# A matrix read whole in the last pair of a first pass, and a place of their own for the first operands of the second pass

## The chip, the cores and the metric

The kernel runs on one core of a Trainium2 chip. The metric is the device time of one execution, in microseconds (us). A core has a TensorE (PE: matrix products, with its weight loads listed apart as PEld), a VectorE (DVE), a ScalarE (ACT), a GpSimd (POOL) and a SyncE (SP), which here does nothing but issue DMAs, one after the other. Each engine works through its own list of instructions in order, and waits for others by semaphores. DMAs move data between the device memory (HBM) and the on-chip memories.

## What is computed

One transformer layer with a spatial gate, x of 2048 rows and 512 columns, all in float32:

```python
x = A_x
h = x + _A_ref(_layernorm(x, axis=-1), A_wqkv, A_wo)       # softmax attention, 32 heads of 16
h2 = h + _B_ref(_layernorm(h, axis=-1), B_w_in, B_w_sp, B_b_sp, B_w_out)

def _B_ref(x, w_in, w_sp, b_sp, w_out):                    # F = 1376, Fh = 688
    z = _gelu(jnp.einsum("bsd,df->bsf", x, w_in))
    z1 = z[..., :Fh]
    z2 = _layernorm(z[..., Fh:], axis=-1)
    g = jnp.einsum("ts,bsf->btf", w_sp, z2) + b_sp[None, :, None]
    return jnp.einsum("bsf,fd->bsd", z1 * g, w_out)
```

The change lies in the second half: the gate product `w_sp @ z2` (2048 x 2048 by 2048 x 688) and the last product with `w_out` (688 x 512).

## The kernel before

Every float32 product is made of three products of a high and a low part: a matrix is split into `hi` (a rounded copy) and `lo` (the rest), and `mm3` (L86-L90) issues hi·hi, hi·lo and lo·hi. `parts` (L757) splits for the gate stage: the copy on ACT (L762), the subtraction on DVE (L763).

The stages are: the projections; the attention (512 units, L674-L738, with a hand-written order of the engines and of SP); the stage `mid`, which makes h, z1 and z2 and stores them in HBM (`h_scr`, `z_scr`); and `fin` (from L867), the gate.

`fin` computes the gate product in the manner of Strassen and Winograd with seven half-size products. A pair `p` (0 to 7) is the row block p of the upper half and the row block p + 8 of the lower half.

- **First pass** (L903-L965): for each pair four products g7, g6, g4, g5, 24 matmuls each. `keep` (L907) makes three sums of them on DVE and stores them to `g_scr[p]` with SP (L910). The operands made of z2 stand in the tiles `T["t3"]`, `T["t2"]`, `T["n4"]`, `T["t1"]`, each as a high and a low tile, of the pool `zc`; the operands made of `w_sp` rotate through six slots of 128 x 2048 (tags w0 to w2 of pool `wc`, f0 to f2 of pool `fin_s`). In the last pair (`last`) the operands of the second pass are made as well: `a11`, `s4`, `a12` into slots f0 to f2, the rest of `b11`, and `b22` and `b21` (8 blocks each, by `load_b`, L880, and `put_b`) in the places of t3 and t2. `load_b` takes its six staging buffers in turn, three of pool `fin_1` and three with the tag `hn` of pool `early_2` (`e2`).
- **Second pass** (L1034-L1086, order of PE, ACT and DVE written by hand): for each pair three products g1, g3, g2; the sums that `fetch` (L978) loads from `g_scr` are added, the result `pr` (a top and a bottom row block, `top` and `bot`) is multiplied with z1, turned (transposed on PE, L1010, split into `pT` by L80 and L85) and multiplied with `w_out` (`wu`, 18 matmuls of 512 columns), h is added and the rows stored. `fetch(p)` loads the sums `q`, the gate rows `z1`, the rows `h`, and for p > 0 `a11`, `a12` and `s2` of `w_sp`. `fetch(0)` and `fetch(1)` are called ahead of the loop's first products.

Pools are places in the on-chip memory. `wc`, `e2` and `fin_1` belong to `late`, which is closed (L972) between the passes; the pool `fin_2` of the second pass takes the memory that they leave. An instruction that writes a tile of `fin_2` therefore waits until everything that read or wrote the old tiles in that memory is done, DMAs too. The tiles `q`, `z1`, `h`, `a11`, `pr` and `pT` of the second pass are all of `fin_2`.

`w_out` is split during the attention: for each of its six row blocks `split_wu` (L660) loads it and splits it on POOL, `store_wu` (L669) stores both parts into `w_scr` in HBM. In the last pair of the first pass the two parts of the first five blocks are loaded from `w_scr` into the place of `n4` (L957-L962), and those of the last block of 48 rows (L968-L971) into the place of the high tile of `t1`.

SP's issue order in `fin` is the scheduler's. Between the passes it is:

```
wu high part, keep(1) store, wu low part, keep(2) and keep(0) stores, wu last block x2,
fetch(0): q, z1[0], h[0], z1[1], h[1]
fetch(1): q, a11 x2, a12 x2, s2 x2, z1[0], h[0], z1[1], h[1]
fetch(2): q, ...
```

Of the kernel before, what the change touches and what calls it, by code (L numbers as in the profile page):

```python
# [8 lines left out]
F32 = mybir.dt.float32  # L9
F32R = mybir.dt.float32r  # L10
# [8 lines left out]
P = 128  # L19
S = 2048  # L20
D = 512
H = 32
DH = 16
FH = 688
# [3 lines left out]
HB = NB // 2  # L28
# [10 lines left out]
FB = [(i * P, min(P, FH - i * P)) for i in range(6)]  # L39
FC = FH // 2  # L40
# [4 lines left out]
def block_kernel(ctx: ExitStack, tc: tile.TileContext, x, wqkv, wo, w_in, w_sp4, b_sp, w_out, out):  # L45
# [7 lines left out]
    nc = tc.nc  # L53
# [3 lines left out]
    dram = ctx.enter_context(tc.tile_pool(name="dram", bufs=1, space=DRAM))  # L57
# [14 lines left out]
    z_scr = [dram.tile([S, FH], F32, name=f"z{i}_scr") for i in range(2)]  # L72
    s_scr = dram.tile([HB, P, HB, P], F32, name="s_scr")
    g_scr = [dram.tile([3, P, FC], F32, name=f"g{p}_scr") for p in range(HB)]
    w_scr = dram.tile([2, FH, D], F32, name="w_scr")

    def split(hi, lo, src, eh=None, el=None):

        if eh == "act":
            nc.scalar.activation(hi, src, AF.Copy)  # L80
        elif eh == "pool":
            nc.gpsimd.tensor_copy(hi, src)  # L82
        else:
            nc.vector.tensor_copy(hi, src)
        (nc.gpsimd if el == "pool" else nc.vector).tensor_sub(lo, src, hi.bitcast(F32))  # L85
# [161 lines left out]
    with ExitStack() as pre:  # L247
# [163 lines left out]
        with tc.manual_schedule(engines={E.PE, E.Activation, E.DVE, E.SP}):  # L411
# [47 lines left out]
            for g in range(3):  # L459
                a, b = 4 * g, 4 * g + 4  # L460
# [44 lines left out]
            for j in range(24):  # L505
                b, n, i = 1 + j // 8, j // 2 % 4, 1 - j % 2
# [28 lines left out]
    wc = late.enter_context(tc.tile_pool(name="wc", bufs=1))  # L535
    e2 = late.enter_context(tc.tile_pool(name="early_2", bufs=2))
# [54 lines left out]
    with ExitStack() as at:  # L591
# [65 lines left out]
            nc.sync.dma_start(t, src[:, a, f])  # L657
            split(dst[0][:, a, f], dst[1][:, a, f], t, "pool", "pool")

        def split_wu(i):  # L660

            f0, fn = FB[i]
            t = e2.tile([P, D], F32, name="wu", tag="hn", bufs=3)
            nc.sync.dma_start(t[:fn], w_out[f0:f0 + fn, :])
            wus[:] = [e2.tile([P, D], F32R, name=f"wu{j}", tag=f"o2{j}", bufs=1) for j in range(2)]
            split(wus[0][:fn], wus[1][:fn], t[:fn], "pool", "pool")

        def store_wu(i):
            f0, fn = FB[i]  # L669
            for j in range(2):  # L670
                nc.sync.dma_start(w_scr[j, f0:f0 + fn, :], wus[j][:fn].bitcast(F32))

        wus = []

        units = [(hg, qb, kb) for hg in range(HG) for qb in range(NQ) for kb in range(NB)]
        prev, turn, later = None, [0], []
        with tc.manual_schedule(engines={E.PE, E.Activation, E.DVE, E.SP}):
            for n in range(0, len(units), 2):
                (hg, qb, kb), (_, _, kb1) = units[n:n + 2]
                if hg + 1 < HG and n % 64 < 24 and n % 4 == 0:  # L680
                    load_k(hg + 1, [n % 64 // 4])
                if hg + 1 < HG and n % 64 < 12 and n % 4 == 2:
                    load_uv(hg + 1, [n % 64 // 4])
                if hg + 1 < HG and n % 64 == 30:
                    load_v(hg + 1)
                if kb == 2 and n // NB + 3 < HG * NQ:
                    load_q(n // NB + 3)
                steps = max_pair(m) if m < 8 * HG * NQ else []
                m += 1
                if not steps and not later:  # L690
                    maxima.close()
                    later.append(attn.enter_context(
                        tc.tile_pool(name="ps_l", bufs=1, space=PSUM, side="right")))
                step = lambda b: steps and steps.pop(0)(b)
                pts = [score(hg, qb, kb, 0), score(hg, qb, kb, 1)]
                step(2)
                step(0)
                if prev is None:

                    pv[0] = ps_v.tile([P, 512], F32, name="pv")  # L700
                    for j in range(4):
                        nc.tensor.matmul(pv[0][32 * j:32 * j + 32, :], vst[0][:, :32],
                                         vst[0][:, :512], start=True, stop=True)
                else:
                    weigh(*prev)
                step(1)
                if kb == 0 and n:
                    gather(*units[n - 1][:2])
                step(2)
                pts1 = [score(hg, qb, kb1, 0)]  # L710
                step(0)
                pts1.append(score(hg, qb, kb1, 1))
                step(1)
                step(2)
                weigh(hg, qb, kb, pts)
                if turned:
                    max_rows()
                step(1)
                prev = (hg, qb, kb1, pts1)
                if kb == 6 and n > NB:  # L720
                    invert()
                if n % 32 == 16 and n < 6 * 32:
                    load_weights(n // 32)
                if 6 * 32 <= n < 12 * 32:
                    if n % 32 == 16:
                        split_wu(n // 32 - 6)
                    if n % 32 == 26:
                        store_wu(n // 32 - 6)
                if n in (498, 502, 506):
                    load_o(h_rows[(n - 498) // 4])  # L730
                if n in (502, 506):
                    split_o(h_rows[(n - 502) // 4])
                if n in (504, 508):
                    make_h(h_rows[(n - 504) // 4], later[0].tile([P, 512], F32, name="h"), True)
            weigh(*prev)
            gather(*prev[:2])
            invert()
# [5 lines left out]
    zc = ctx.enter_context(tc.tile_pool(name="zc", bufs=1, side="right"))  # L743
# [14 lines left out]
    def parts(hi, lo, src, el=None, eh=None):  # L758
        if eh == "pool":
            nc.gpsimd.tensor_copy(hi, src)  # L760
        else:
            nc.scalar.activation(hi, src, AF.Copy)  # L762
        (nc.gpsimd if el == "pool" else nc.vector).tensor_sub(lo, src, hi.bitcast(F32))  # L763
# [36 lines left out]
    with ExitStack() as mid:  # L800
# [56 lines left out]
        w = [Slot(wc, f"w{i}") for i in range(3)]  # L857
# [15 lines left out]
    with ExitStack() as fin:  # L873
# [8 lines left out]
        def load_b(i, j, k):  # L882

            t = (f1.tile([P, FC], F32, name="b", bufs=3) if k % 2 else
                 e2.tile([P, FC], F32, name="b", tag="hn", bufs=3))
            nc.sync.dma_start(t, z_scr[1][(HB * i + k) * P:(HB * i + k + 1) * P, j * FC:(j + 1) * FC])
            return t
# [14 lines left out]
        for p in range(HB):  # L902
# [17 lines left out]
            put_b(b11, p, load_b(0, 0, p))  # L920
            if last:
                bs = [load_b(1, 1, k) for k in range(6)]
            if p:
                product(g7, ops["s3"], T["t3"])
            else:
                for blocks in (range(HB - 1), range(HB - 1, HB)):
                    product(g7, ops["s3"], T["t3"], blocks)
                    product(g6, ops["s2"], T["t2"], blocks)
# [26 lines left out]
            keep(1, g4, p67)  # L955
            if last:

                wu = [zc.tile([P, HB * FC], F32R, name="wu", tag=f"n4_{i}")[:, :5 * D].rearrange(
                    "p (a c) -> p a c", c=D) for i in range(2)]
                for i in range(2):  # L960
                    nc.sync.dma_start(wu[i].bitcast(F32),
                                      w_scr[i, :5 * P, :].rearrange("(a p) c -> p a c", p=P))  # L962
            product(g5, ops["s1"], T["t1"])
            keep(2, g5, p67)
            keep(0, g5, p6)  # L965
            ops, old, now = nxt, now, new
        fn = FB[-1][1]
        t = zc.tile([P, HB * FC], F32R, name="wu5", tag="t1_0")  # L968
        wu = [[w[:, i, :] for i in range(5)] + [t[:fn, j * D:(j + 1) * D]] for j, w in enumerate(wu)]
        for i in range(2):  # L970
            nc.sync.dma_start(wu[i][5].bitcast(F32), w_scr[i, 5 * P:, :])  # L971
        late.close()  # L972


# [2 lines left out]
        def fetch(p):  # L977

            rows = [slice((p + HB * i) * P, (p + HB * i + 1) * P) for i in range(2)]
            half = lambda n: [f2.tile([P, QB, P], F32, name=n) for _ in range(2)]  # L980
            q = f2.tile([P, 3, FC], F32, name="q")
            nc.sync.dma_start(q, g_scr[p].rearrange("i p c -> p i c"))
            raw = None
            if p:
                raw = [half("a11"), half("a12"), half("s2")]
                load_a(raw[0], 0, 0, p)
                load_a(raw[1], 0, 1, p)
                for n in range(2):
                    nc.sync.dma_start(raw[2][n], cut(s_scr[p])[n])
            z1 = [f2.tile([P, FH], F32, name=f"z1{i}") for i in range(2)]  # L990
            h = [f2.tile([P, D], F32, name=f"h{i}") for i in range(2)]
            for i in range(2):
                nc.sync.dma_start(z1[i], z_scr[0][rows[i], :])
                nc.sync.dma_start(h[i], h_scr[rows[i], :])
            return q, raw, z1, h

# [119 lines left out]
```

## Time and profile before

| what | us |
|---|---|
| three runs, median (lowest to highest) | 1916.77 (1914.2 to 1917.29) |
| the profiled execution, its own time | 1915.51 |
| its span, first to last instruction | 1913.7 |
| PE busy | 1881.6 (98%) |
| DVE busy | 1532.8 (80%) |
| ACT busy | 1326.3 (69%) |
| POOL busy | 215.5 (11%) |

The span runs from the first to the last instruction; the execution's own time is 1.8 us longer. The page cuts the span in 40 equal slices of 47.8 us and gives each engine's busy share of a slice as a digit (9 is 90% or more). PE's digits are 9 in all slices but one near the end. The matmuls are pipelined, so the start-to-start distance of two, and not the listed length of one, says how fast PE goes. PEclk is the clock granted to PE (1.00 is full).

The first pass and the second pass lie one behind the other in the last sixth of the span: in the profiled execution the last product of the first pass ends at 1714.9 us, and the second pair of the second pass starts at 1751.07 us.

### The profile page before, as it was taken

The page shows a single profiled execution, that of the slowest core. Times are in us where ns is not written, and L with a number is a line of the kernel's source. Part 1 is how long each engine was busy: PE and PEld are TensorE (multiplying, and loading weights), DVE is VectorE, ACT ScalarE, POOL GpSimd, SP SyncE. Part 2 cuts the span into 40 slices and gives each one's busy share as a digit, 9 for nine tenths or more (in the row PEclk, how much of TensorE's full clock was granted, in tenths as well). Part 3 has the DMA queues.
Part 4 walks back from the last instruction along what each step waited for, and adds up shares of the span by engine and source line. Part 5 has one row for each costly group of instructions (what it writes and reads, how often), then busy time and mean ns, then how long its engine had stood idle before and what let it go on. Part 6 is the DMA issues. An engine that isn't in the chain of part 4 may idle for free. (4 is left out here: it accounts for less than half of the span.)

```text
span 1913.7 us, 32477 instructions
## 1 busy us (share of the span) xinstructions
PE 1881.6 (98%) x11608; PEld 1067.1 (56%) x11608; DVE 1532.8 (80%) x3101; ACT 1326.3 (69%) x1729; POOL 215.5 (11%) x293
## 2 busy tenths in 40 slices
PE   9999999999999999999999999999999999996999
PEld 6765444444444444444444444444349899995887
DVE  6487999999999999999999999999536677674554
ACT  3335888888888888888888888888964345342221
POOL 2130000001011000000000000000015551001211
PEclk9999999999999999999999999999999999998999
DMA  5677111210221111121122021000045556657550
GB/s 187 185 196 184 40 24 31 70 26 28 49 51 32 38 45 27 52 46 35 35 56 44 15 53 32 22 13 5 7 106 156 160 171 206 199 182 257 181 181 34
DMA packets 151161, 165.46 MB, mean 86 GB/s; under 512 B 63256, under 2 KB 92968, under 8 KB 149464
## 3 DMA queue, kind: packets, MB, share of 16 engines
q1 hardware_dynamic: 146360, 152.11, 29.6%
q10 hardware_dynamic: 4608, 11.27, 1.5%
q8 instruction: 91, 1.49, 0.3%
q14 instruction: 70, 0.57, 0.1%
q0 software_dynamic: 32, 0.01, 0.0%
HBM read 103.98 MB, written 58.43 MB: 85 GB/s over the span
## 5 line engine op out<-in xcount | busy, mean ns | idle before, releaser
L612 ACT ACTIVATE pt<-s 128x1024 f32<-128x1024 f32 x1024 | 992.9, 1029 | 144.4 <-PE s L609 142.1
L209 DVE TENSOR_REDUCE mx<-m 128x1 f32<-128x512 f32 x1511 | 958.1, 683 | 105.6 <-PE m L204 62.3
L204 PE MATMUL m<-kst,qst 48*128 48x512 f32 x1511 | 607.5, 448 | 0.0
L620 PE MATMUL pv<-pt,vst 128*32 128x512 f32 x4096 | 550.8, 605 | 0.4 <-ACT o L627 0.4
L609 PE MATMUL s<-qst,kst 50*128 50x512 f32 x2048 | 465.9, 428 | 2.9 <-ACT pt L612 2.3
L204 PEld LDWEIGHTS m<-kst,qst 48*128 48x128 f32 x1511 | 263.5, 184 | 314.9 <-DVE mx L209 221.2
L609 PEld LDWEIGHTS s<-qst,kst 50*128 50x128 f32 x2048 | 223.0, 185 | 57.2 <-ACT pt L612 32.6
L204 PE MATMUL m<-uvs,qst 48*128 48x512 f32 x503 | 248.9, 495 | 0.0
L204 PEld LDWEIGHTS m<-uvs,qst 48*128 48x128 f32 x503 | 91.8, 183 | 207.2 <-DVE mx L209 205.3
L218 DVE CUSTOM_DVE_ANT_0 ab<-m,ab 128x512 f32<-128x512 f32 x252 | 171.2, 679 | 3.8 <-ACT ab L214 2.0
L620 PEld LDWEIGHTS pv<-pt,vst 128*32 128x32 f32 x4096 | 82.9, 108 | 161.6 <-issue 155.6
L214 ACT ACTIVATE ab<-m 128x512 f32<-128x512 f32 x251 | 150.9, 601 | 16.8 <-PE m L204 16.3
L82 POOL CAST mparts<-nm 128x16 fp32r<-128x16 f32 x32 | 6.3, 198 | 749.9 <-DVE nm L224 749.9
L762 ACT ACTIVATE ws<-a 128x512 fp32r<-128x512 f32 x80 | 46.6, 625 | 60.8 <-issue 26.7
L88 PE MATMUL acc<-wi,hT 128*128 128x344 f32 x256 | 82.9, 324 | 0.0
L89 PE MATMUL acc<-wi,hT 128*128 128x344 f32 x256 | 81.8, 320 | 0.0
L90 PE MATMUL acc<-wi,hT 128*128 128x344 f32 x256 | 81.8, 319 | 0.0
L763 DVE TENSOR_TENSOR ws<-a,ws 128x512 fp32r<-128x512 f32 x80 | 55.8, 741 | 14.4 <-ACT ws L762 14.4
L88 PE MATMUL g<-b,ws 128*128 128x344 f32 x192 | 65.0, 338 | 0.0
L80 ACT ACTIVATE pT<-tp 128x384 fp32r<-128x384 f32 (+2 forms) x48 | 18.4, 382 | 66.4 <-PE tp L1010 49.0
L88 PE MATMUL g<-t,ws 128*128 128x344 f32 x192 | 61.4, 320 | 0.6 <-issue 0.6
L89 PE MATMUL g<-b,ws 128*128 128x344 f32 x192 | 61.9, 322 | 0.0
(185 smaller groups left out, 2179.2 us busy)
## 6 DMA issues: line engine op xcount, KB each, us to landing
a<-in_w_sp SPq DMA_DIRECT2D x80, 256.0 KB
qst<-q_scr SPq DMA_DIRECT2D x192, 64.0 KB
kst<-k_scr SPq DMA_DIRECT2D x48, 256.0 KB
z_scr<-z ACTq DMA_DIRECT2D x32, 344.0 KB
k_scr<-part SPq DMA_DIRECT2D x16, 512.0 KB
q_scr<-part SPq DMA_DIRECT2D x16, 512.0 KB
z<-z_scr SPq DMA_DIRECT2D x16, 344.0 KB
b<-z_scr SPq DMA_DIRECT2D x24, 172.0 KB
```

The lines of the kernel that those rows point to most:

```text
L88: nc.tensor.matmul(ps, lh, rh, start=first, stop=False)
L89: nc.tensor.matmul(ps, lh, rl, start=False, stop=False)
L90: nc.tensor.matmul(ps, ll, rh, start=False, stop=last)
L204: nc.tensor.matmul(acc, q[r, p, c], keys[r, p], start=True, stop=True)
L209: nc.vector.reduce_max(at(t, e if t else e - 1), acc, axis=AX.X)
L214: nc.scalar.activation(ab[0], acc, AF.Abs)
L218: nc.vector.tensor_tensor_reduce(ab[0], acc, ab[0], 0.5, LOW, ALU.add, ALU.max, at(0, 0))
L609: nc.tensor.matmul(s[:, t, :], k[r, p, kb * P:(kb + 1) * P], q[r, p, :], start=True, stop=True)
L612: nc.scalar.activation(t, s, AF.Exp, scale=DH ** -0.5)
L620: nc.tensor.matmul(pv[0][32 * j:32 * j + 32, :], vst[hg % 2][:, c:c + 32], pts[j % 2][:, j // 2, :], start=kb == 0, stop=kb == NB - 1)
L762: nc.scalar.activation(hi, src, AF.Copy)
L763: (nc.gpsimd if el == "pool" else nc.vector).tensor_sub(lo, src, hi.bitcast(F32))
```

## The change

The splitting of `w_out` during the attention, with its scratch tensor in HBM, is taken out. In the last pair of the first pass `w_out` is loaded as it is: the first four row blocks by one DMA into the slot w2, the last two by one DMA each into buffers with the tag `rc` of `e2`. It is split with `parts` into the same places as before, the first two blocks ahead of the product g5, the rest behind the first pass. The sums and the z1 rows of `fetch(0)` get a place of their own, the low tile of `t1`, instead of tiles in `fin_2`. In `fetch` the z1 rows are loaded straight behind the sums, the lower row block first, and h comes last, the lower first too.

```diff
-    w_scr = dram.tile([2, FH, D], F32, name="w_scr")
...
-        def split_wu(i):
-
-            f0, fn = FB[i]
-            t = e2.tile([P, D], F32, name="wu", tag="hn", bufs=3)
-            nc.sync.dma_start(t[:fn], w_out[f0:f0 + fn, :])
-            wus[:] = [e2.tile([P, D], F32R, name=f"wu{j}", tag=f"o2{j}", bufs=1) for j in range(2)]
-            split(wus[0][:fn], wus[1][:fn], t[:fn], "pool", "pool")
-
-        def store_wu(i):
-            f0, fn = FB[i]
-            for j in range(2):
-                nc.sync.dma_start(w_scr[j, f0:f0 + fn, :], wus[j][:fn].bitcast(F32))
...
-                if 6 * 32 <= n < 12 * 32:
-                    if n % 32 == 16:
-                        split_wu(n // 32 - 6)
-                    if n % 32 == 26:
-                        store_wu(n // 32 - 6)
...
             if last:
                 bs = [load_b(1, 1, k) for k in range(6)]
+
+                raw_u = wc.tile([P, 4, D], F32, name="wr", tag="w2")
+                nc.sync.dma_start(raw_u, w_out[:4 * P, :].rearrange("(a p) c -> p a c", p=P))
+                raw_u = [raw_u[:, :2, :], raw_u[:, 2:, :]]
...
             keep(1, g4, p67)
             if last:
 
+                for f0, n in FB[4:]:
+                    t = e2.tile([P, D], F32, name="wr", tag="rc")
+                    nc.sync.dma_start(t[:n], w_out[f0:f0 + n, :])
+                    raw_u.append(t[:n])
                 wu = [zc.tile([P, HB * FC], F32R, name="wu", tag=f"n4_{i}")[:, :5 * D].rearrange(
                     "p (a c) -> p a c", c=D) for i in range(2)]
-                for i in range(2):
-                    nc.sync.dma_start(wu[i].bitcast(F32),
-                                      w_scr[i, :5 * P, :].rearrange("(a p) c -> p a c", p=P))
+                parts(wu[0][:, :2, :], wu[1][:, :2, :], raw_u[0])
             product(g5, ops["s1"], T["t1"])
...
         t = zc.tile([P, HB * FC], F32R, name="wu5", tag="t1_0")
+        wu_places = [[w[:, 2 * i:2 * i + 2, :] for w in wu] for i in range(2)]
+        wu_places += [[w[:, 4, :] for w in wu], [t[:fn, j * D:(j + 1) * D] for j in range(2)]]
         wu = [[w[:, i, :] for i in range(5)] + [t[:fn, j * D:(j + 1) * D]] for j, w in enumerate(wu)]
-        for i in range(2):
-            nc.sync.dma_start(wu[i][5].bitcast(F32), w_scr[i, 5 * P:, :])
+        for i in range(1, 4):
+            parts(*wu_places[i], raw_u[i])
+        t = zc.tile([P, HB * FC], F32, name="qz", tag="t1_1")
+        first = (t[:, :3 * FC].rearrange("p (i c) -> p i c", c=FC),
+                 [t[:, (3 + 2 * i) * FC:(5 + 2 * i) * FC] for i in range(2)])
         late.close()
...
-            q = f2.tile([P, 3, FC], F32, name="q")
+            q, z1 = first if not p else (f2.tile([P, 3, FC], F32, name="q"),
+                                         [f2.tile([P, FH], F32, name=f"z1{i}") for i in range(2)])
             nc.sync.dma_start(q, g_scr[p].rearrange("i p c -> p i c"))
+            for i in (1, 0):
+                nc.sync.dma_start(z1[i], z_scr[0][rows[i], :])
             raw = None
...
-            z1 = [f2.tile([P, FH], F32, name=f"z1{i}") for i in range(2)]
             h = [f2.tile([P, D], F32, name=f"h{i}") for i in range(2)]
-            for i in range(2):
-                nc.sync.dma_start(z1[i], z_scr[0][rows[i], :])
+            for i in (1, 0):
                 nc.sync.dma_start(h[i], h_scr[rows[i], :])
```

In the program built from it, SP's order between the passes is: `w_out` (four blocks), the three stores of pair 6, `w_out` (the last two blocks), ten `load_b`, the keep(1) store, `fetch(0)`'s q, the keep(2) and keep(0) stores, `fetch(0)`'s z1 x2 and h x2, then `fetch(1)`: q, z1 x2, a11 x2, a12 x2, s2 x2, h x2, then `fetch(2)`. The first split of `w_out` (128 x 1024) stands on DVE between the sixth and the seventh block of b21, on ACT between the fifth and the sixth, with a second one behind the sixth; the rest of them stand behind the last block of b21, on DVE behind the sums of keep(0). PE's order is as before.

More of the change, by code (lines that the diff above doesn't have):

```diff
@@ L658, in load_weights @@
             split(dst[0][:, a, f], dst[1][:, a, f], t, "pool", "pool")
-        def split_wu(i):
-            f0, fn = FB[i]
-            t = e2.tile([P, D], F32, name="wu", tag="hn", bufs=3)
-            nc.sync.dma_start(t[:fn], w_out[f0:f0 + fn, :])
-            wus[:] = [e2.tile([P, D], F32R, name=f"wu{j}", tag=f"o2{j}", bufs=1) for j in range(2)]
-            split(wus[0][:fn], wus[1][:fn], t[:fn], "pool", "pool")
-        def store_wu(i):
-            f0, fn = FB[i]
-            for j in range(2):
-                nc.sync.dma_start(w_scr[j, f0:f0 + fn, :], wus[j][:fn].bitcast(F32))
-        wus = []
         units = [(hg, qb, kb) for hg in range(HG) for qb in range(NQ) for kb in range(NB)]
```

## The prediction

> **What bounds the kernel now.** I read the slices first, to find where PE is not full; then the work by stretches of 20 and of 3 us there; then PE's waits; then the chain of waits through that place.
>
> ```profile
> PE   9999999999999999999999999999999999996999
> ...
> PEclk9999999999999999999999999999999999998999
> ```
>
> PE sets the time everywhere but in slice 36 (1722 to 1770 us), the seam between the two passes; its clock is lower there too. In stretches (us; then PE, PEld, DVE, ACT, POOL busy with counts; granted clock; DMA share; GB/s):
>
> ```profile
> 1700.00:1720.00 20.00, 20.00 (x129) 20.00 (x129) 16.11 (x34) 10.30 (x23) 0.00 (x0) 1.00 0.65 183
> 1720.00:1740.00 20.00, 7.89 (x43) 7.58 (x42) 3.33 (x6) 1.76 (x3) 0.00 (x0) 0.71 0.88 299
> 1740.00:1760.00 20.00, 16.72 (x72) 12.89 (x70) 11.08 (x21) 6.07 (x13) 4.51 (x3) 0.87 0.75 256
> 1760.00:1780.00 20.00, 20.00 (x115) 18.02 (x115) 11.53 (x20) 4.81 (x11) 3.42 (x3) 1.00 0.57 188
> ```
>
> While PE stands, the DMA engines are the busy ones. PE's longest waits in the gate stage:
>
> ```profile
> PE tp L1010 <- DVE pr L1048: 12.1, 1, 12.1
> PE acc L88 <- ACT pT L80: 3.8, 2, 3.2
> ```
>
> PE runs out at 1724.4 (its 60 products of the second pass that need no `pr`, from 1714.9, at 0.157 us each), waits 12.1 us for the first `pr`, turns it at 1736.54, runs the second half of g2, and waits 3.2 us for `pT` until 1744.70. Pair 1 starts at 1751.07. The chain (start, us, what):
>
> ```profile
> 1716.12 0.44 DVE q L909
> 1716.57 0.32 SPq L910
> 1716.94 1.77 SPq L961
> 1718.81 0.67 SPq L910
> 1719.58 9.19 DMA g_scr<-q
> 1728.85 0.38 SPq L982
> 1729.29 0.48 SPq L993
> 1729.81 0.43 SPq L994
> 1730.28 5.08 DMA z<-z_scr
> 1735.38 7.45 DMA s<-s_scr
> 1742.92 0.70 DVE s L782
> 1743.64 0.64 ACT ws L762
> ```
>
> The last `g_scr` store takes 9.19 us, because the 2.8 MB of `wu` issued around it share the DMA engines. Only then may q(0) be loaded (L982): its tile lies where the stored sums lay. Then comes z1[1] (L993), which frees the first wait, and s2 of pair 1, which frees the second: on ACT and DVE the split of pair 1's s4 stands ahead of the `pT` split. The second wait is so a refill by DMA: 14.0 us from q(0)'s issue at 1728.85 to s2's landing at 1742.83.
>
> **The change, part by part.**
>
> *Attention.* 12 POOL instructions go (six of 0.61 and six of 1.29 us, 11.4 us) and 18 DMA issues of SP. The beat of the attention, from one `mparts` of POOL to the next, starts at 666.95, 705.97, 745.07, 784.09, 823.16: 39.02 with a `wu` split in it, 39.10 without, 39.02 with, 39.07 without. The splits were hidden under PE and cost nothing; bounds -0.5 to +0.5 us over six. I take 0.
>
> *Loads of w_out in the last pair.* 1.05 MB is issued behind the `w_sp` loads that end at 1702.3; its slot w2 was last read by pair 6's g4, done at 1696.1, so SP does not wait. Queued behind it are the stores of pair 6, the last two blocks (0.36 MB, which wait for the split of a11 at 1706 to 1707.3) and ten `load_b`, the first of which waits for a DVE split at 1707.7 anyway. The DMA engines moved 153 to 203 GB/s between 1702 and 1708 and 399 elsewhere (1738 to 1741), so there is room. Lower bound 0; upper bound 1.41 MB at 158 GB/s (the stretch 1726 to 1729), 8.9 us. I take 0.5 us on the chain of `load_b`, since room is there.
>
> *Splits of w_out.* One 128 x 1024 on DVE ahead of the last sums: twice 0.60 us (the step from one 128 x 512 L763 to the next), 1.2 us; on ACT two of 1.05 (two L762 of 128 x 512: 1.14). By the order of the two engines b21's last two blocks end at 1719.1 in place of 1717.85, and keep(0) at 1720.0 in place of 1718.7; with the 0.5 above, 1720.5. The other splits (1.2, 0.6 and 0.6 on DVE) run until 1723, while the stores land. If that cover is gone they cost up to 2.4 us.
>
> *Stores of the sums.* Issued at 1720.6 to 1721. They no longer stand among 2.8 MB, only q(0)'s 0.53 MB. Bounds: 2.0 us (a `load_b` issued at 1714.4 is used at 1716.39) and 9.19. I take 2.4: landed at 1723.2. The Trainium skill ("DMA: Bandwidth & Descriptors", "Latency and other measured facts") puts the fixed cost of a DMA at about 2 us, largest when HBM is loaded; with 2.0 in place of 2.4 the sum would be 0.4 us lower.
>
> *q(0) and z1(0).* q(0) is issued behind keep(1)'s store at about 1717.3 (its place is free since g5's end at 1714.9) and lands, with the 4.1 us of before (1728.85 to 1732.95), at 1721.4. z1 follows the last store: issued 1721.0, with 3 to 5.08 us landed at 1724 to 1726. But `pr` still lies in `fin_2`, so the first DVE sum still waits for the stores: 1723.2. Three sums 1.54, the multiplication 0.88: PE turns at 1726.0 in place of 1736.54. First gap: 1.6 in place of 12.1 us.
>
> *The refill.* h(0) is now the first load that waits for the stores: 1723.2. Behind it SP issues h, q(1), z1 x2, four loads of `w_sp` and s2 x2, some 0.47 us each; all of pair 1's preparation waits for them. From h(0)'s issue to s2 0.52 + 0.53 + 0.70 + 1.05 + 0.52 = 3.3 MB, and 0.70 of z1(0) issued 2.2 us earlier: 4.0 MB; before, 3.85 MB in 14.0 us. Counted from z1(0)'s issue: 1721.0 + 14.0 x 4.0/3.85 = 1735.6; counted from h's alone 1723.2 + 14.0 x 3.3/3.85 = 1735.2; a11 in the middle, by its own 11.1 us from a11's issue (1731.75) to s2's landing, now issued at 1725.4, 1736.5. I take 1736.0 (bounds under the rivals).
>
> *Behind it* the steps stay: 1.87 us from s2's landing to PE (1742.83 to 1744.70), and 6.37 us for `bot`'s 18 products. Nine of these run at 0.43 us and nine at 0.235, as before, because PE has then stood from 1728.5 to 1737.9, and the clock fell within 4 us of standing (1.00 until 1726, 0.87 in 1726 to 1729, 0.50 after). Pair 1 starts at 1736.0 + 1.87 + 6.37 = 1744.2 in place of 1751.07: **6.8 us less**. From there all is as before; only pair 2's z1 are loaded ahead of its `w_sp`, 0.7 MB, and these are needed 7 us into pair 1.
>
> Sum: 0 (attention) - 10.5 (first gap) - 2.5 (the turn and g2's second half at full clock: 0.57 + 12 x 0.157 in place of 4.95) + 6.2 (second gap, 9.4 in place of 3.2) = -6.8. Of the profiled execution's 1915.51 (span 1913.7 and 1.8 around it) that leaves 1908.7. The median of the runs shown stands 1.3 us higher; I forecast **1909.0**.
>
> **The rivals.**
>
> *B, a fast refill.* Nothing but pair 1's operands is left to load, and 399 GB/s was moved at 1738 to 1741 and 402 behind it. 3.3 MB and 0.3 MB left of z1 at 399 take 9.0 us; from 1723.2 with 1.5 us until data flows s2 lands at 1733.7 or sooner: gain 9.1 to 11, 1905. Against it: SP issues each load alone, and before the rate was 169 GB/s in the first 3 us. The Trainium skill ("DMA: Bandwidth & Descriptors", "Where 436 GB/s comes from") sets 358 GB/s for one core's share of HBM; the trace went above that, so the row decides; with 358 B would gain 1.1 us less.
>
> *C, the stall moves whole.* The `load_b` chain ends 2 us later still, z1(1)'s 0.7 MB ahead of a11 and s2 count in full, and s2 lands 14.0 us behind the first load that `fin_2` lets go, but at 1725.2: 1739.2 to 1740. Gain 2.8 to 3.6, 1912.4.
>
> *D, slower: w_out ahead of the ten `load_b`.* Place: the loop DVE, SP, DMA, ACT, DVE through six buffers in the last pair. The sum p67 of pair 7 (1711.84) stands behind b22's last blocks, and g1 needs its bank at 1714.9, so 3 us are free; past that PE stands and the stores, the refill and pair 1 follow. It eats the gain when b22's block 6 is 7.3 us later than before (1710.06), and is a loss over 0.2% from 11 us on: 1.41 MB at 128 GB/s or less. With 14 us (100 GB/s) the end comes 6.7 us later: 1922. Against it: 153 to 248 GB/s flowed here already.
>
> *E, it doesn't do what it says.* The places help q and z1 but `pr` stays behind the stores. If these still take 9.19 us (then the cause isn't `wu`), they land at 1729.8, h is issued where q(0) was, and 1915.2 comes out. For it: nothing but the overlap shows the cause. Against it: 300 and 388 GB/s were flowing at 1720 to 1726, and the stores are 0.35 MB.
>
> **How the numbers follow.** Forecast 0.56 (own range 1906 to 1911.7), B 0.15, C 0.11, E 0.08, D 0.10. About 0.2%, 3.8 us, is what a measurement of this kernel can tell from no change. Faster by more: the forecast, B and a fifth of C, 0.73; within: the rest of C, E, a little of the other two, 0.17; slower: D, 0.10. The range 1903.5 to 1914 leaves out E, D and the far ends.
>
> **What would show it.** Right: the `g_scr` store landing in 2 to 3 us; PE's wait for L1048's successor under 3 us at 1724 to 1727; a wait of 8 to 10 us for the `pT` split ending at 1737 to 1739; PE full in the attention as before. Wrong: p67 of pair 7 later than 1714.9 (D), stores of 9 us (E), a `pT` wait of 12 us or more (C) or under 7 (B), or a gap of PE where there was none.

## The result, and the profile after

| | before | changed |
|---|---|---|
| median of 8 runs (lowest to highest), us | 1916.32 (1914.2 to 1917.29) | 1910.62 (1908.08 to 1914.73) |
| ratio to before, 95% interval | | 0.9973 (0.9962 to 0.9984) |
| the profiled execution: own time, span | 1915.51, 1913.7 | 1914.12, 1912.3 |

The kernel became faster by 5.2 us by the ratio (3.1 to 7.3), 5.7 us by the medians. The profiled execution of the changed kernel, 1914.12 us, is the second slowest of its eight. The same kernel was measured once more later (label after_again: ratio 0.9974, 0.9965 to 0.9984; median 1910.84, 1908.32 to 1914.27; its profiled execution 1909.47), and the two profiles together show what varies.

The slices of the changed kernel's page:

```profile
span 1912.3 us, 32432 instructions
...
PE   9999999999999999999999999999999999997999
...
PEclk9999999999999999999999999999999999998999
```

The seam is still the only place where PE is not full. The work by stretches (columns as before the prediction):

```profile
1700.00:1720.00 20.00, 17.29 (x102) 17.01 (x101) 12.73 (x26) 8.73 (x21) 0.00 (x0) 0.92 0.67 202
1720.00:1740.00 20.00, 12.19 (x68) 11.63 (x66) 11.43 (x21) 5.82 (x10) 0.05 (x1) 0.84 0.88 292
1740.00:1760.00 20.00, 16.89 (x74) 13.43 (x75) 11.36 (x20) 5.98 (x13) 4.44 (x3) 0.81 0.59 204
```

PE does 4.3 us more in 1720 to 1740 and 2.7 us less in 1700 to 1720: a hole has opened ahead of the old one. PE's waits (total, times, longest):

```profile
PE acc L87 <- ACT pT L79: 9.5, 2, 8.9
PE g L87 <- ACT p L924: 2.7, 1, 2.7
...
PE tp L1001 <- ACT pr L1038: 2.0, 1, 2.0
```

The 12.1 us for the first `pr` are down to 2.0. The wait for `pT` grew from 3.2 to 8.9, as worked out. New is 2.7 us at the first product of the second pass, which waits until ACT has read g6 of pair 7 (L924). The chain of waits of this execution (start, us, what) says why:

```profile
1709.07 6.70 DMA b<-z_scr
1715.79 0.49 ACT b L741
...
1724.15 0.85 DVE q L888 x2
...
1726.66 0.68 DVE wu L742
1727.36 0.32 SPq L985
...
1732.69 7.26 DMA s<-s_scr
1740.05 1.37 DVE s L761
1741.50 1.17 ACT ws L741 x2
1742.67 0.39 ACT pT L79
```

One `load_b`, b22's block 6, takes 6.70 us (2.3 before: issued at 1707.76, used at 1710.06). ACT's reading of g6 and DVE's p67 stand behind it, so PE waits, and the last sums of the pass are ready at 1725.0 instead of 1718.7. Then the split of `w_out` ends (1727.3), h(0) is issued at 1727.36, and 12.6 us later s2 of pair 1 has landed (1739.95), which frees the `pT` split.

In the second profile of the same kernel the same steps stand:

```profile
PE acc L87 <- ACT pT L79: 9.0, 2, 8.4
PE tp L1001 <- DVE pr L1039: 3.5, 1, 3.5
```

and in its chain

```profile
1705.42 6.26 DMA b<-z_scr
...
1720.07 0.85 DVE q L888 x2
...
1728.38 6.92 DMA s<-s_scr
```

The `load_b` is as slow (6.26 us), but it was issued 3.6 us earlier, while PE's first pass ended only 1.1 us earlier, and PE did not run into it. So the late `load_b` is there in both profiles, and whether PE has to wait for it depends on how far DVE and PE are apart by then. Of the 4.9 us between the two spans, 3.8 us lie in the seam and 1.1 us ahead of it. How much of the spread of the other runs (6.7 us in all) comes from this isn't shown.

### The profile page after: what moved, and what is told of

It is laid out like the page before. It is cut to its first block, busy times and chain, and to the rows that moved or that the text cites. A ratio compares the mean times of both kernels' runs of the same rounds, so it can differ in the third digit from the quotient of the medians.

```text
span 1912.3 us, 32432 instructions
## 1 busy us (share of the span) xinstructions
PE 1883.8 (99%) x11608; PEld 1068.5 (56%) x11608; DVE 1535.9 (80%) x3105; ACT 1328.8 (69%) x1733; POOL 203.9 (11%) x281
## 5 line engine op out<-in xcount | busy, mean ns | idle before, releaser
L213 ACT ACTIVATE ab<-m 128x512 f32<-128x512 f32 x251 | 151.2, 602 | 16.7 <-PE tp L203 10.5
L87 PE MATMUL g<-b,ws 128*128 128x344 f32 x192 | 65.7, 342 | 2.7 <-ACT p L924 2.7
L88 PE MATMUL g<-b,ws 128*128 128x344 f32 x192 | 62.5, 326 | 0.0
L89 PE MATMUL g<-b,ws 128*128 128x344 f32 x192 | 62.4, 325 | 0.0
```

The source lines that it names most:

```text
L87: nc.tensor.matmul(ps, lh, rh, start=first, stop=False)
L88: nc.tensor.matmul(ps, lh, rl, start=False, stop=False)
L89: nc.tensor.matmul(ps, ll, rh, start=False, stop=last)
L213: nc.scalar.activation(ab[0], acc, AF.Abs)
```

## The experiments

All compare with runs of the kernel before on the same chip. The seam of each profile, from PE's order in time, runs from the end of the first pass (the last product with t1) to the start of pair 1's first product. Each row but its median is of one execution, whose own time stands in the second column from the right.

| kernel | `load_b` of b22[6], us | wait for first pr | wait for pT | seam | from pair 1 to the end | this execution, us | median, us |
|---|---|---|---|---|---|---|---|
| before | 2.3 | 12.1 | 3.2 | 36.2 | 162.6 | 1915.5 | 1916.3 |
| changed | 6.7 | 2.7 + 2.0 | 8.9 | 35.9 | 162.6 | 1914.1 | 1910.6 |
| after_again | 6.3 | 3.5 | 8.4 | 32.2 | 162.5 | 1909.5 | 1910.8 |
| place_only | 2.35 | 12.3 | 5.9 | 39.5 | 162.7 | 1918.1 | 1915.6 |
| wout_only | 5.3 | 9.4 | 4.1 | 33.9 | 162.5 | 1914.5 | 1911.25 |
| wout_half | 2.8 | 0 | 9.2 | 27.3 | 162.5 | 1909.4 | 1912.7 |
| wout_late | 2.25 | 10.3 | 8.3 | 39.3 | 162.5 | 1913.8 | 1916.4 |
| before_pt | 2.4 | 13.0 | 0 | 32.1 | 162.6 | 1911.1 | 1908.6 |
| wout_pt | 5.9 | 6.8 | 0 | 25.8 | 162.5 | 1903.1 | 1903.5 |
| pt_first | 6.3 | 2.5 | 0 | 20.7 | 163.8 | 1899.9 | 1901.5 |

From pair 1 on nothing differs by more than 1.3 us: all that these kernels win or lose lies ahead of it. The end of the first pass itself moved between 1710.2 and 1717.8 over these profiles, which is why the seam, and not one execution's total, is compared. Most of that movement is older than the first pass: its first product started between 1589.7 (wout_late) and 1595.9 (wout_only), in kernels whose code is the same up to there. The pass itself took 120.4 to 120.6 us in each of them but wout_half, where it took 127.1.

**place_only**: the kernel before with the own place and the new order of `fetch` alone.

```diff
+        t = zc.tile([P, HB * FC], F32, name="qz", tag="t1_1")
+        first = (t[:, :3 * FC].rearrange("p (i c) -> p i c", c=FC),
+                 [t[:, (3 + 2 * i) * FC:(5 + 2 * i) * FC] for i in range(2)])
...
-            q = f2.tile([P, 3, FC], F32, name="q")
+            q, z1 = first if not p else (f2.tile([P, 3, FC], F32, name="q"),
+                                         [f2.tile([P, FH], F32, name=f"z1{i}") for i in range(2)])
             nc.sync.dma_start(q, g_scr[p].rearrange("i p c -> p i c"))
+            for i in (1, 0):
+                nc.sync.dma_start(z1[i], z_scr[0][rows[i], :])
...
-            z1 = [f2.tile([P, FH], F32, name=f"z1{i}") for i in range(2)]
             h = [f2.tile([P, D], F32, name=f"h{i}") for i in range(2)]
-            for i in range(2):
-                nc.sync.dma_start(z1[i], z_scr[0][rows[i], :])
+            for i in (1, 0):
                 nc.sync.dma_start(h[i], h_scr[rows[i], :])
```

> Only the own place for q(0) and z1(0) and the new order of fetch; w_out goes through w_scr as before. Refill theory (what ends the seam is the moment at which the memory of the late pools is let go, plus 14 us of loads): the stores still share the DMA engines with 2.8 MB and land about 9 us after their issue, h(0) is issued at 1728 to 1729, s2 of pair 1 lands at 1741 to 1742, PE's wait for the first pr falls from 12.1 to about 7 us and the wait for pT grows to 6 to 8: gain 0 to 2 us, 1914 to 1916. Place theory (the freed place of q and z1 is what shortens the seam): gain 5 us or more, about 1910.

Measured: ratio 1.0001 (0.9990 to 1.0011), median 1915.58. PE's waits, DVE's first sums for `pr` (start, length, in brackets the wait ahead of them), and two steps of its chain:

```profile
PE tp L1014 <- DMA q<-g_scr: 12.3, 1, 12.3
PE acc L88 <- ACT pT L80: 6.5, 2, 5.9
```

```profile
1733.44 1.54 DVE L1050 SCALAR_TENSOR_TENSOR pr<-g,bias,qz 128x344 f32<-128x344 f32 x3 [13.13 <-DMA qz<-g_scr]
```

```profile
1721.64 9.45 DMA g_scr<-q
...
1736.29 7.40 DMA s<-s_scr
```

With 2.8 MB of `wu` around them the stores take 9.45 us again, and h(0) is issued when they have landed, at 1731.17. The first sums of `pr` start only at 1733.44: they wait for q(0) itself. Its place was free, but its load was issued at 1723.25, behind the stores and `wu`, and landed some 10 us later. So in this kernel the own place lets q(0) be issued before the stores land, and wins nothing, since the load stands behind the same bytes. The expectation of 7 us for the first wait was too good (12.3; its last sums and stores were also 2 us later than in the profile before). The total is the refill theory's, and a gain of 5 us by the place alone is ruled out. What the place is worth without `wu` in the way, this run can't say; wout_only and wout_pt below, which leave it out, can.

**wout_only**: the changed way of `w_out` alone; q(0), z1(0) and `fetch` as before.

> Only the way of w_out is changed (loaded whole in the last pair, split there); q(0), z1(0) and fetch as before. Refill theory: the stores land 2 to 4 us after their issue, q(0) is loaded at once behind them, the first pr comes some 4 us later than with the own place, but s2 lands about 14 us behind the release all the same: gain 4 to 6 us, 1910 to 1912. Place theory: no gain, 1916 or slower by the splits, 1917.

Measured: 0.9973 (0.9961 to 0.9986), median 1911.25. The whole gain of the change comes from this part.

```profile
PE tp L997 <- DVE pr L1035: 9.4, 1, 9.4
PE acc L87 <- ACT pT L79: 4.6, 2, 4.1
```

The first wait is 6 to 7 us longer than with the own place (9.4 against 3.5 and 2.0), the second 4 to 5 us shorter, and the seam of 33.9 us lies between the two of the changed kernel: the place moves time from one wait to the other, since s2 of pair 1 ends the seam in both.

**wout_half**: three blocks of `w_out` loaded early into `fin_1`, 0.62 MB in the last pair.

```diff
+            if p == 2:
+                raw_e = f1.tile([P, 3, D], F32, name="wre", bufs=1)
+                nc.sync.dma_start(raw_e, w_out[:3 * P, :].rearrange("(a p) c -> p a c", p=P))
...
-                nc.sync.dma_start(raw_u, w_out[:4 * P, :].rearrange("(a p) c -> p a c", p=P))
+                nc.sync.dma_start(t[:, :2, :], w_out[3 * P:5 * P, :].rearrange("(a p) c -> p a c", p=P))
+                nc.sync.dma_start(t[:FB[-1][1], 2, :], w_out[5 * P:, :])
```

> The changed kernel, but three of w_out's row blocks are loaded during pair 2 into a buffer of fin_1, and only 0.62 MB instead of 1.41 MB is issued in the last pair ahead of the ten load_b. If w_out ahead of the load_b is what makes PE wait 2.7 us at the start of the second pass and delays the last sums by 5 us: that wait is gone or under 1 us, the load_b issued at 1709 lands in 2 to 4 us instead of 6.7, median 1906 to 1909 with a narrower spread. If the splits or the load_b themselves are the cause: the same as the changed kernel, 1910 to 1911, with the wait.

Measured: 0.9981 (0.9970 to 0.9992), median 1912.73; 1906 to 1909 was expected. The seam did what was expected, the total did not.

```profile
PE acc L87 <- ACT pT L79: 9.2, 1, 9.2
PE g L89 <- DVE ws L742: 3.8, 1, 3.8
```

```profile
1709.21 3.44 DMA b<-z_scr
...
1720.96 1.84 DMA g_scr<-q
```

The load of b22[6], issued at 1708.79, is in use 2.85 us later, the one behind it lands in 3.44 us (the row above), the wait at the start of the second pass and the wait for the first `pr` are gone, and the seam is 27.3 us. But PE has a new wait of 3.8 us in the first pass, until 1610.06, for a split of `w_sp`: the early load was issued at 1590.45, as the pass began, ahead of `w_sp` that this pass needed. No other profile here but half_pt's, which loads in the same way, has that wait. And it costs more than its length, as the work by stretches ahead of it and behind it shows (columns as before):

```profile
1600.00:1606.00 6.00, 6.00 (x40) 5.97 (x39) 4.00 (x8) 4.50 (x11) 0.00 (x0) 1.00 0.57 153
1610.00:1616.00 6.00, 5.94 (x21) 5.94 (x22) 6.00 (x13) 0.45 (x2) 0.00 (x0) 0.51 0.69 212
```

In the 6 us behind the wait the granted clock was 0.51, and PE did 21 products in place of 40. The first pass took 127.1 us in place of 120.4, so 6.7 us went where 4.9 to 8.6 were won against the two profiles of the changed kernel. The price moved.

**wout_late**: `w_out` into slots that come free behind the last pair's a22 and s1, all splits behind the pass.

```diff
-                raw_u = wc.tile([P, 4, D], F32, name="wr", tag="w2")
...
             keep(0, g5, p6)
+            if last:
+                raw_u = wc.tile([P, 4, D], F32, name="wr", tag="w1")
+                nc.sync.dma_start(raw_u, w_out[:4 * P, :].rearrange("(a p) c -> p a c", p=P))
```

> The changed kernel, but w_out is loaded into the slots w0 and w1, which come free only at the end of the pass, so behind all ten load_b and the stores, and split whole behind the last sums. If w_out issued ahead of the load_b is what delays them: the load_b lands in 2.0 to 2.6 us, PE does not wait for p6 at the start of the second pass, the last sums are ready by 1719 to 1720. The splits then end the release instead: they wait for 1.05 MB issued behind the stores, the first pr comes at about 1727, and the total is that of the changed kernel, 1909 to 1913. If the load_b are late for another reason: they take 5 to 7 us here too.

Measured: 0.9996 (0.9983 to 1.0008), median 1916.39; 1909 to 1913 was expected.

```profile
1704.77 2.25 DMA b<-z_scr
...
1716.17 7.74 DMA wr<-in_w_out
```

The `load_b` is at its old 2.25 us with nothing ahead of it, which settles what delays it in the changed kernel. The other half was mis-sized: the 1.05 MB behind the stores took 7.74 us, the splits waited for them, and h(0) was issued 17.2 us behind the end of the first pass (13.6 and 10.6 in the two profiles of the changed kernel). The gain is gone: the interval holds 1.

**pt_first**: the changed kernel; in pair 0 of the second pass the splits of pair 1's a11 and s4 are ordered behind `pT`'s.

```diff
-                if not last:
+                if p and not last:
                     a11 = put(f[0], nxt[1][0])
...
-                if not last:
+                if p and not last:
                     combine(nc.vector, nxt[1][2], nxt[1][1], nxt[1][2], ALU.subtract)
                     s4 = put(f[1], nxt[1][2])
...
                 (nc.vector if last else nc.gpsimd).tensor_mul(left, left, z1[0][:, :FC])
+                if not p:
+                    a11 = put(f[0], nxt[1][0])
+                    combine(nc.vector, nxt[1][2], nxt[1][1], nxt[1][2], ALU.subtract)
+                    s4 = put(f[1], nxt[1][2])
```

> The changed kernel, but in pair 0 of the second pass the splits of pair 1's a11 and s4 are ordered behind the split of pT on ACT and DVE. If the second wait (8.9 us for pT) is only this order, it goes: pT is split as soon as PE has turned pr, and pair 1 starts when a11 is split, 9 us earlier: 1900 to 1904. If the DMA refill bounds in any order: the wait moves to pair 1's first product (waiting for a11) with the same end, gain over the changed kernel under 3 us, 1908 to 1911.

Measured: 0.9923 (0.9905 to 0.9942), median 1901.52, and again in a later group (pt_first_b, expected below) 0.9913 (0.9889 to 0.9936), median 1899.20. The stretches:

```profile
1700.00:1720.00 20.00, 20.00 (x129) 20.00 (x128) 14.53 (x30) 12.85 (x27) 0.00 (x0) 1.00 0.75 229
1720.00:1740.00 20.00, 17.08 (x89) 14.72 (x87) 13.55 (x24) 5.64 (x11) 1.84 (x2) 0.91 0.98 337
```

PE is busy through the seam but for the first wait of 2.5 us, and the DMA engines are as busy as in after_again (0.98 and 0.99 in 1720 to 1740): the refill now runs beside PE. s2 still lands 12 us behind h(0). All that PE still waits behind it is 0.8 us within pair 1, for a `pT` split that stands behind s4's on DVE, and that is part of the 1.3 us by which the stretch from pair 1 to the end is longer. The second wait was an order, not a lack of bandwidth.

**before_pt** and **wout_pt**: the same order in the kernel before, and in wout_only.

> The kernel before, with the splits of pair 1's a11 and s4 ordered behind the split of pT in pair 0. If the second wait stands behind the first one in both kernels, this takes only the 3.2 us wait away: PE still waits 12 us for the first pr, turns it at 1736, and pair 1 starts at about 1747 in place of 1751: 1912 to 1913.5. If the order of these splits were the whole cause of the seam: 1902 as with the changed kernel.

> The changed way of w_out without the own place of q(0) and z1(0), with the pT split first. If the own place shortens only the first wait, and this was hidden under the refill as long as the pT split stood behind s4, it counts now: the first pr needs q(0) and z1(0) loaded behind the release, PE turns it 4 to 5 us later than with the own place, 1905 to 1907. If the place is worth nothing in any order: 1901 to 1902, as with it.

Measured: before_pt 0.9967 (0.9954 to 0.9980), median 1908.57; wout_pt 0.9942 (0.9925 to 0.9958), median 1903.49. before_pt won more than expected in the median; its profile is as expected (the first wait 13.0, no wait for `pT`, pair 1 at 1746.4), and the interval reaches down to the 4 us expected. wout_pt lies between its two expectations. In its profile the own place begins to count: the first wait is 6.8 us against 2.5 with it, and the seam 25.8 against 20.7. The medians, 1903.5 against 1901.5 and 1899.2, say 2 to 4 us, but the intervals overlap (0.9925 to 0.9958 against 0.9905 to 0.9942 and 0.9889 to 0.9936), so a gain of the place in the total isn't clear of the noise.

**pt_first_b, pt_a11, half_pt**: what is left of the seam. pt_a11 loads a11 ahead of the sums and z1 in `fetch`; half_pt is pt_first with wout_half's loads.

> The version with the pT split first once more, beside the next two: 1900 to 1903.

> The version with the pT split first, and fetch loads a11 ahead of the sums and z1. With the pT split first nothing on PE waits for a11 any more (pair 1 starts without a wait), so this should change nothing: within 1 us of the version without it. If a11 still sets pair 1's start, 2 us or more are gained.

> The version with the pT split first, and three of w_out's blocks loaded at the start of the first pass. If the price of w_out's load only moves (3.8 us of PE's wait at the start of the first pass in place of the later load_b and the first wait of the seam): 1900 to 1903, no gain over the version without it. If the load in the last pair is what is left to win: 1897 to 1899.

Measured: 1899.20, 1899.64 (0.9916, 0.9891 to 0.9942) and 1900.65 (0.9916, 0.9889 to 0.9944). pt_first_b came out 0.8 us under what was expected. Neither of the other two changes anything that can be told from it. half_pt's profile has a seam of 16.4 us, against 20.1 in pt_first_b's, and pays for it with the wait in the first pass again: 3.9 us, and a pass of 126.1 us.

pt_first beats both kernels, by 15 to 17 us against before and 9 to 11.5 against the changed one. Alone, the change is worth 5.2 us and the order of the splits 6.3; together 14.8 and 16.7 in the two groups. Two waits stand in series. The change alone cuts the first and lets the second grow, from 3.2 to 8.4 and 8.9 us; the order alone takes the second away and leaves the first, 13.0 us; together 2.5 us are left.

## Why the prediction was right, point by point

- *Attention at nothing:* right. The beat of `mparts` in the changed kernel is 38.96 to 39.10 us, with no split in it; over eleven beats (666.35 to 1095.60) it is 0.2 us shorter than before.
- *`load_b` 0.5 us later:* the term of the sum that was mis-sized. It measured 4.0 to 4.4 us more (6.26 and 6.70 against 2.3), and 5.3 to 6.3 us in the other kernels with that load. The reading of "room" was from a mean rate; a short load does not use the room but stands behind the bytes that were issued ahead of it. With 0, 0.62 and 1.41 MB ahead it took 2.25 to 2.4, 2.8 and 5.3 to 6.7 us. This is rival D's mechanism at two fifths of the 11 us from which it would have made the kernel slower, and two of the prediction's own signs of being wrong came in the first profile: p67 of pair 7 at 1717.47, later than 1714.9, and a gap of PE, 2.7 us, where there was none. What PE waited for there was ACT's reading of g6 (1716.18), ahead of p67, which the prediction had named. In the second profile p67 stood at 1713.39, PE did not wait, and the late load only made the release later.
- *Splits 1.2 us, the rest hidden under the stores:* the sizes are right (1.21 and 2.41 us on DVE), but the cover was fully used: SP's h(0) is issued 0.03 us behind the last split in both profiles, so the splits, not the stores, end the release.
- *Stores in 2.4 us:* right, 1.84 us in wout_half and at most 2.4 in the two profiles of the changed kernel. Rival E falls; place_only shows its premise, 9.45 us, where `wu` stays. The Trainium skill ("DMA: Bandwidth & Descriptors", "Latency and other measured facts") gives 2 us of memory access at high load; beside 2.8 MB in the same queue the landing was 9.2 to 10.3 us here, so the bytes in the queue decide.
- *First gap 1.6 us:* 2.0 and 3.5. The sign of being right, under 3 us at 1724 to 1727, was met in length by the first profile (which ended it at 1729.92) and in time by the second (1725.78).
- *Refill 12.8 us from h(0)'s issue to s2:* right, 12.6 and 12.0. Rival B needed 10.5 or less, C 14.0. *Second gap 9.4:* right, 8.9 and 8.4.
- *Pair 1 at 29.3 us behind the first pass:* 32.2 and 35.9, by the lateness of the `load_b` chain. So the seam became shorter by 4.0 and 0.3 us, where 6.9 were forecast, and the median of 1910.6 is nearer to the 1909.0 than the parts are. The profile of 1909.47 us gets there because its first pass also ended 2.2 us earlier than in the profile before (in the other, 1.1 us). Where the first pass starts moved by 6 us among kernels that are alike up to there, so no share of the change in this is shown, and the prediction gave none: to that extent the number is luck. How the 5.2 us of the median divide between the seam and what lies ahead of it stays open.
- *Which part does it:* the prediction gave the first gap's 10.5 us to the own place and the missing `wu` together. wout_only and place_only show that `wu` leaving the stores alone is worth all of the 5 us, and the own place nothing that can be measured. It moves time from the second wait to the first; only with the `pT` split freed from s4 does the profile show a shorter seam by it.
- What was not seen: that the second wait could be taken away by the order of DVE and ACT. The prediction named the cause (s4's split stands ahead of `pT`'s) and counted it as a refill by DMA all the same.

## What to carry to other kernels

Price a transfer that is put ahead of small loads by its bytes at the full rate, as an upper estimate, and follow the small loads into the instructions that stand behind them on each engine; a mean DMA share says nothing of it. Price a new wait of PE by more than its length: here 3.8 us of it cost 6.7. When a wait is removed, ask of the next one whether its data is late or whether a ready instruction stands behind one that isn't: here 9 us of "waiting for DMA" were an order of two splits. Compare two profiles of one kernel before one execution's total is explained.

## What the runs showed of the hardware

A store of 176 KB landed in 1.84 us (wout_half, beside q(0)'s load of 0.53 MB) and in 9.2 to 10.3 us beside 2.8 MB of loads (before, place_only, before_pt).

A load of 176 KB took 2.25 to 2.4 us with none of `w_out` ahead of it, 2.8 with 0.62 MB and 5.3 to 6.7 with 1.41 MB. At the 324 to 342 GB/s at which the DMA engines ran in 1710 to 1716 of the first profile, 1.41 MB take 4.1 to 4.4 us by estimate, and 3.0 to 4.4 us more were measured. By the same rate 0.62 MB take 1.8 to 1.9 us, and only 0.5 us more were measured there, so the bytes ahead are an upper estimate and not a rule.

Behind PE's wait of 3.8 us in wout_half the granted clock was 0.51 for 6 us.
